# A transformer layer on one core: the first stage ordered by hand, seven v tiles and a Q block moved into later dense groups

## The chip, the cores and the metric

The kernel runs on 1 core of one Trainium2 chip, in one launch. The metric is device time in microseconds of the whole program. One profiled execution of the program comes with a trace of every instruction on the five engines: PE (TensorE), DVE (VectorE), ACT (ScalarE), POOL (GpSimd) and SP (SyncE, which issues nearly all DMAs here).

## The reference

```python
# S = 2048 rows, D = 512, H = 32 heads of 16, F = 1792; all float32
xn  = layernorm(x)                              # eps 1e-5, no scale, no shift
q, k, v = heads(xn @ wqkv)                      # wqkv: 512 x 1536
p   = softmax(q @ k.T / 4)                      # per head, 2048 x 2048
A   = merge(p @ v) @ wo
B   = gelu_tanh(xn @ w1 + b1) @ w2 + b2
out = x + A + B
```

## The kernel before

**Numbers.** Operands of the dense products are split into a float16 high and low half, each scaled by a power of two found from the largest absolute value of a weight; a product is three matmuls per slice of 128 (`PAIRS`). A dense 512-wide result is therefore 12 products (q, k, v, hidden layer), or 21 for half of the second MLP matrix.

**Attention in units.** Heads come in eight groups of four (`NG`), queries in four blocks of 512 (`NQB`), keys in 16 tiles of 128: 8 x 4 x 16 = 512 units (`NU`). Unit `u` has two sides that run 20 units apart (`LEAD`). The score side (`s_half`, four times a unit) multiplies four 32-column tiles of queries with 512 keys and takes the row maximum on DVE into `mt`; this is only there to find each row's maximum. After 16 units (`s_end`, `store`, `put`) the negated maxima go through DRAM into two spare rows of the stacked queries `qst`; the matching rows of the stacked keys `kst` hold 1024 (`MROW`). The value side (`e_half`, `v_half`) makes the transposed scores with the maximum already subtracted, takes the exponential on ACT and multiplies with `vv`, the v rows with a column of ones for the sum. `stacks` loads `kst` and `qst` from `qk_d` in DRAM, where the projections stored them.

**PE in halves.** In the steady part the array is used in two halves of 64 rows and four columns of tiles. While `v_half` runs on one row half, `dense` puts products of the current `Group` on the other: `pace` says how many half-width parts a unit's half gets, `FAST` 8, `MEAN` 7, `SLOW` 6. A 12-product group is 48 parts: three units at FAST, four at SLOW. Groups are given by generators: `rest` (the q and k projections of head blocks `m` = 1 to 3), then `mlp` (hidden groups at SLOW, sums at MEAN), then `tail` (the product with `wo`). Before unit 20, where no value side runs yet, `unit` calls `burst`, which puts `LFILL` whole products on the full array twice a unit.

**First stage.** Up to unit 16 the code is not run by `unit`: `stats` makes the mean and inverse deviation of four x tiles and normalises them, `transpose_x` turns x into `xt`, `prep_qk` and `prep_v` scale and split weights, `project` makes q and k of head block 0, `v_proj` all 16 v tiles, and `tile_and_unit` interleaves one score unit with one v tile (two score blocks, six products, two blocks, six products). `measure` finds the largest absolute values of w1, w2 and wo, half a 512 KB chunk at a time; chunks rotate over three buffers (`chunk`, `fetch`). In this stage the order on each engine is the planner's; from `rest` on (`manual_schedule`) it is the order of the code. SP's DMA issues stand in one queue, in order.

**Banks.** PSUM has eight banks in named lists: `S` three for scores, `T` three for transposed scores and early work, `D` one for dense groups, `V` one.

**Weights of the MLP.** `prepare` runs beside the units from 17 on: it finishes `measure`, forms scales, loads every chunk again, and splits it on POOL (`split_steps`, three operations a chunk) into `w1_d`, `w2_d` and `wo_s`.

Of the kernel before, what the change touches and what calls it, by code (L numbers as in the profile page):

```python
# [17 lines left out]
P = 128  # L18
# [14 lines left out]
MEASURE = (3, 0, 1, 2)  # L33
# [4 lines left out]
LFILL = 6  # L38
# [5 lines left out]
MROW = 1024.0  # L44
W = 2 * P
# [3 lines left out]
def layer_kernel(ctx: ExitStack, tc: tile.TileContext, x, wqkv, wo, w1, b1, w2, b2, out):  # L49
# [7 lines left out]

    const = pool(ctx, "const")
# [18 lines left out]
    ones_row = const.tile([2, P], F16, name="ones_row")  # L77
    nc.vector.memset(ones_row, MROW)

# [4 lines left out]
    def clear(i):  # L84
        for b in range(NQB):
            for p in range(2):
                for st in (kst[i][p][b], qst[i][p][b]):
                    nc.gpsimd.memset(st.bitcast(F32), 0.0)
                for a in range(2):
                    nc.sync.dma_start(kst[i][p][b][64 * a + 62:64 * a + 64, :].rearrange("r (b n) -> r b n", n=P),  # L90
                                      ones_row.unsqueeze(1).to_broadcast([2, 4, P]))
# [254 lines left out]
    def v_half(u, a):  # L346

        t, kt = divmod(u, 16)
        g, qb = divmod(t, NQB)
        if kt == 0 and a == 0:  # L350
            pv_of[t] = hold("V", "S")
        pv = pv_of[t][0]
        r = slice(64 * a, 64 * a + 64)
        for h in (2, 3, 0, 1):
# [91 lines left out]
    def dbank():  # L446
        turn[0] += 1
        if pos[0] < LEAD:
            return banks("T"), None
# [62 lines left out]
    def prep_qk(m, wf, bank, ready_w):  # L512
# [5 lines left out]
        yield from scales(am, 2, bank, box) if m < 2 else spread_scales(m, am, box)  # L518
        inv, fac = box
        wh = ph.tile([P, 2, 2, NC, P], F16, name="wqk_h", bufs=2)  # L520
        for w in (1, 0):
            (split if w and m == 0 else split_pool)(wh[:, w, 0], wh[:, w, 1], wf[w], inv[:, w:w + 1])
            yield
        nc.vector.tensor_tensor(sexp[:, m:m + 1], fac[:, 0:1], fac[:, 1:2], op=ALU.mult)
# [14 lines left out]
    def project(m, w, sb, wh, bank, early=False):  # L539
# [6 lines left out]
        def finish(pj):  # L546
# [21 lines left out]
            put()  # L568

# [9 lines left out]
    def v_proj(t, wh, bank):  # L579
        pj = bank()  # L580
        n = 0
        for c in range(NC):
            for i, j in PAIRS:
                nc.tensor.matmul(pj, xt[:, i, c, t * P:(t + 1) * P], wh[j][:, c, :], start=(n == 0), stop=(n == 11))  # L584
                n += 1
                yield 1.0
        nc.scalar.activation(vv[:, t, 0:H * VW].rearrange("p (h e) -> p h e", e=VW)[:, :, 0:DH],
                             pj.rearrange("p (h d) -> p h d", d=DH), AF.Copy)

# [78 lines left out]
    def unit(gen):  # L668
# [4 lines left out]
        if u == LEAD and cur[0] is not None:  # L673
            burst(gen, cur[0].left())
        pos[0] += 1
# [37 lines left out]
    with ExitStack() as st1:  # L713
# [23 lines left out]

        b1_s = const.tile([P, NF], F32, name="b1_s")
# [6 lines left out]
        amx = work.tile([P, 16, 2], F32, name="amx")  # L745
        fac1 = []
# [17 lines left out]
        def stats(sb):  # L764
# [20 lines left out]
            for i in range(4):  # L785
                v = xs[4 * sb + i]
                if sb and i >= 2:
# [12 lines left out]
        def transpose_x(sb, c):  # L800
            cs = slice(sb * QB, (sb + 1) * QB)
            pt = vbank()
            for i in range(4):
                nc.tensor.transpose(pt[:, i * P:(i + 1) * P], xs[4 * sb + i][:, c * P:(c + 1) * P], ident)
            nc.scalar.activation(xt[:, 0, c, cs], pt, AF.Copy)
            if sb and c % 2:
# [5 lines left out]
            if c == NC - 1:  # L812
                for t in range(4 * sb + 8, min(4 * sb + 12, NT)):
                    load_x(t)
# [19 lines left out]
        def measure():  # L834

            for n in range(16):
                v = fetch(n)
                for k in range(2):
                    absmax(amx[:, n, k:k + 1], v[:, 2 * k:2 * k + 2, :] if n < 7 else v[:, k, :])
                    yield  # L840
# [7 lines left out]
        def tile_and_unit(t):  # L848

            if t < 8:  # L850
                keep_x(t)
            v = v_proj(t, wvh, vbank)
            for k in range(2):
                s_half(t, 2 * k)
                s_half(t, 2 * k + 1)
                some(v, 6)
            s_end(t)
            run(v)
# [16 lines left out]
        def pq3(gen):  # L875
            for _ in range(3):
                next(gen)
                yield

        clear(0)  # L880
        ln, pq, pv = stats(0), prep_qk(0, wfs[0], sbank, ready_w), prep_v()
        warm(WARM[0])
        some(ln, 5)
        some(pq, 2)
        warm(WARM[1])
        some(ln, 3)
        some(pq, 1)
        some(ln, 2)
        weave(pq3(pq), ln)
        transpose_x(0, 0)  # L890
        warm(WARM[2])
        some(pq, 1)
        transpose_x(0, 1)
        warm(WARM[3])
        transpose_x(0, 2)
        transpose_x(0, 3)
        run(pq)
        run(stats(1))
        for w in (1, 0):
            run(whole(project(0, w, 0, ready_w[0], lambda: (vbank(), None), True)))  # L900
        for w in (1, 0):
            stacks(0, w, [0])
        free[:] = ["T", "D", "T", "V", "T"]
        for c in range(NC):
            transpose_x(1, c)
        some(pv, 2)
        for sb in range(1, NQB):
            ln = stats(sb + 1) if sb < 3 else iter(())
            for w in (1, 0):
                pj = whole(project(0, w, sb, ready_w[0], lambda: (vbank(), None)))  # L910
                for n in range(3):
                    some(pj, 4)
                    some(pv, 1)
                    if sb == 2:
                        some(ln, 3)
                run(pj)
            run(pv)
            for w in (1, 0):
                stacks(0, w, [sb])
            wfs.append(load_qk(sb))  # L920
            if sb == 1:
                clear(1)
            for j in range(4):
                tile_and_unit(4 * sb - 4 + j)
                some(ms, MEASURE[sb])
                if sb == 1:
                    some(ln, 4)
                elif sb == 2:
                    transpose_x(3, j)
            if sb == 1:  # L930
                for c in range(NC):
                    transpose_x(2, c)
        pq = prep_qk(1, wfs[1], sbank, ready_w)
        for j in range(4):
            some(pq, 2)
            tile_and_unit(NT - 4 + j)
            some(ms, MEASURE[0])
        run(pq)
# [6 lines left out]
        def rest():  # L945
            for t in range(8, NT):
                later(2 + 3 * (t - 8), lambda t=t: keep_x(t), True)
            for k in range(8):
                later(8 + 4 * k, lambda k=k: stacks(1, 1 - k // 4, [k % 4]), True)
            for m in range(1, 4):  # L950
                while m not in ready_w:
                    yield None
                if m < 3:
                    by_slots(prep_qk(m + 1, wfs[m + 1], sbank, ready_w))
# [17 lines left out]
        def prepare():  # L972
# [5 lines left out]
            nc.vector.tensor_reduce(am[:, 9:10], amx[:, 14:16, :], axis=AX.XY, op=ALU.max)  # L978
            box = []
# [5 lines left out]
            nc.vector.reduce_max(gs[:, 0:1], fac[:, 0:8], axis=AX.X)  # L985
# [39 lines left out]
        ctx.enter_context(tc.manual_schedule(engines=ORDERED))  # L1025
# [8 lines left out]
    def mlp():  # L1034
# [35 lines left out]
        def hidden_group(s, f):  # L1070
# [6 lines left out]
            def hidden(hp):  # L1077
# [8 lines left out]
                         dbank, hidden, pace=SLOW)  # L1086
# [184 lines left out]
```

## Time and profile before

| | us |
|---|---|
| three runs | 1472.27, 1474.18 (median), 1475.49 |
| the profiled execution | 1471.34 |
| its span, first to last instruction | 1469.5 |
| first score maximum starts | 37.4 |
| first maximum of unit 16, 20, 80 | 110.9, 124.9, 301.2 |
| last maximum ends | 1396.9 |

Times in a window or a timeline row count from the span's start. A windows row gives the stretch, its length, and the busy time and count of instructions in it, then granted clock of TensorE (1.00 is full), mean share of the 16 DMA engines and GB/s. A groups row gives line, engine, operation, out<-in and count, then busy time and mean ns of one, then idle time of the engine just before them with what ended most of it. A row of the chain of waits gives start, length, engine, tile and line. An instruction that straddles a window's edge is counted in both. L291 is the score matmul, L292 the maximum; L195 is the helper `tiled`/`product` with all half-array matmuls; L343 the exponential; L485 whole-array products of a Group; L584 and L587 the v tile and its read; L734 the weight maximum; L804 to L811 the transposes of x; L177 and L178, L967 to L969 splitting on POOL.

### The profile page before, as it was taken

What the parts mean: (1) busy time and instruction counts of PE and PEld (TensorE: products, weight loads), DVE (VectorE), ACT (ScalarE), POOL (GpSimd) and SP (SyncE); (2) the same over time, 40 slices, a digit from 0 to 9 for tenths busy, and PEclk for the clock granted to TensorE, in tenths of its full rate; (3) what the DMA queues carried; (4) which work ended last, traced back from release to release, by engine and by line L of the source; (5) the groups of instructions that cost most, each with busy time, mean ns of one, the idle gap of its engine ahead of it and who ended that gap; (6) DMA issues with size and microseconds to landing.
All of it is one profiled execution on the core that took longest, in us unless ns stands there. A gap on an engine that the chain in (4) does not pass through costs nothing.

```text
span 1469.5 us, 87300 instructions
## 1 busy us (share of the span) xinstructions
PE 1445.6 (98%) x39753; PEld 928.6 (63%) x39753; DVE 1363.0 (93%) x2340; ACT 1230.0 (84%) x2326; POOL 737.5 (50%) x846
## 2 busy tenths in 40 slices
PE   8999989999999999999999999999999999999998
PEld 4434656666666666666666666666666666666674
DVE  7799998999999999999999999999999999999913
ACT  5325877899899999999998999999999999998884
POOL 4113598747766536556553655456475545551100
PEclk9999999999999999999999999999999999999999
DMA  6466457544111211121121211121101211102342
GB/s 205 154 185 176 137 183 241 171 127 117 59 42 44 88 51 37 45 58 53 38 66 45 63 44 45 30 75 50 56 26 54 78 37 35 29 24 73 112 130 102
DMA packets 118023, 124.30 MB, mean 85 GB/s; under 512 B 29080, under 2 KB 89624, under 8 KB 117652
## 3 DMA queue, kind: packets, MB, share of 16 engines
q1 hardware_dynamic: 117652, 118.72, 26.5%
q8 instruction: 310, 5.08, 1.4%
q14 instruction: 61, 0.50, 0.1%
HBM read 80.87 MB, written 37.60 MB: 81 GB/s over the span
## 4 chain that ended last, share of the span: by engine, by line
PE 90%; POOL 4%; DVE 3%; DMA 1%; issue 1%; ACT 1%; SPq 0%; DVEq 0%; POOLq 0%; ACTq 0%
PE pV L195 25%; PE pD L195 23%; PE pT L195 19%; PE pS L291 18%; PE pS L195 2%; PE pT L584 1%; DVE mt L292 1%; PE pV L584 1%; PE pS L485 1%; POOL wsp L969 1%; PE pT L485 1%; DVE amx L734 0%; PE pD L584 0%; PE pD L485 0%; POOL t L1053 0%
## 5 line engine op out<-in xcount | busy, mean ns | idle before, releaser
L292 DVE TENSOR_REDUCE mt<-pS 128x1 f32<-128x512 f32 x2048 | 1270.0, 682 | 35.5 <-PE pS L291 21.6
L343 ACT ACTIVATE pe<-pT 128x512 f32<-128x512 f32 x2048 | 1105.1, 599 | 133.8 <-PE pS L291 64.7
L195 PE MATMUL pV<-pe,vv 64*32 64x512 f32 x8192 | 1088.1, 599 | 0.5 <-issue 0.2
L195 PE MATMUL pT<-qst,kst 64*32 64x512 f16 x8192 | 658.8, 376 | 3.1 <-ACT pe L343 2.1
L291 PE MATMUL pS<-kst,qst 62*32 62x512 f16 x8192 | 621.6, 378 | 6.2 <-DVE mt L292 4.6
L195 PE MATMUL pD<-xb,wc 64*32 64x512 f16 x5376 | 372.0, 374 | 0.0
L195 PE MATMUL pD<-w_s,g 64*32 64x512 f16 (+1 forms) x6144 | 361.4, 348 | 0.6 <-POOL g L1054 0.4
L291 PEld LDWEIGHTS <-qst 62*32 62x32 f16 x8192 | 250.2, 92 | 136.6 <-issue 38.2
L195 PEld LDWEIGHTS <-kst 64*32 64x32 f16 x8192 | 250.3, 93 | 98.3 <-issue 12.7
L195 PEld LDWEIGHTS <-g 64*32 64x32 f16 x6144 | 197.4, 92 | 87.2 <-POOL g L1055 1.1
L195 PEld LDWEIGHTS <-wc 64*32 64x32 f16 x5376 | 178.3, 91 | 98.0
L195 PEld LDWEIGHTS pV<-pe,vv 64*32 64x32 f32 x8192 | 171.0, 105 | 6.6 <-PE pV L195 2.5
L1082 POOL TENSOR_SCALAR hh<-hh,fac,b_s 128x512 f32<-128x512 f32 x56 | 43.0, 768 | 223.9 <-ACT hh L1080 217.8
L195 PE MATMUL pD<-xt,wqk_h 64*32 64x512 f16 x1920 | 128.7, 375 | 2.3 <-issue 1.5
L1109 POOL TENSOR_TENSOR xa<-xa,yt 128x512 f32<-128x512 f32 x32 | 41.1, 1284 | 89.6 <-ACT yt L1107 89.6
L397 POOL TENSOR_TENSOR osb<-osb,rb 128x512 f32<-128x512 f32 x31 | 39.9, 1287 | 89.3 <-DMA rb<-den_d 86.7
L195 PEld LDWEIGHTS <-wqk_h 64*32 64x32 f16 x1920 | 60.8, 92 | 31.0 <-issue 5.9
L1053 POOL TENSOR_TENSOR t<-t,hh 128x512 f32<-128x512 f32 x56 | 71.8, 1282 | 4.7
L1060 POOL TENSOR_TENSOR t<-t,hh 128x512 f32<-128x512 f32 x56 | 71.8, 1281 | 4.7
L1055 POOL TENSOR_TENSOR g<-t,g 128x512 f16<-128x512 f32 x56 | 65.2, 1164 | 4.6
L1146 DVE SCALAR_TENSOR_TENSOR ac<-pS,gs,ac 128x512 f32<-128x512 f32 x20 | 14.4, 743 | 52.0 <-PE pS L195 40.3
L1058 POOL TENSOR_TENSOR t<-hh 128x512 f32<-128x512 f32 x56 | 58.2, 1040 | 4.1
(144 smaller groups left out, 908.1 us busy)
## 6 DMA issues: line engine op xcount, KB each, us to landing
wch<-in_B_w_dram SPq DMA_DIRECT2D x28, 512.0 KB
wc<-w_d SPq DMA_DIRECT2D x56, 256.0 KB
qk_d<-stg SPq DMA_DIRECT2D x32, 256.0 KB
rb<-den_d SPq DMA_DIRECT2D x31, 256.0 KB
w_d<-wsp SPq DMA_DIRECT2D x28, 256.0 KB
kst<-qk_d SPq DMA_DIRECT2D x128, 48.0 KB
qst<-qk_d SPq DMA_DIRECT2D x128, 48.0 KB
xs<-in_A_x_dram SPq DMA_DIRECT2D x16, 256.0 KB
```

Of the source, the lines that this page charges most:

```text
L195: p = nc.tensor.matmul(*args, **kw)
L291: nc.tensor.matmul(s[32 * j:32 * j + 32], qs[p][qb][r, c:c + 32], ks[p][kb][r, :], start=True, stop=True)
L292: nc.vector.reduce_max(mt_of[t][:, n, qt, kb:kb + 1], s, axis=AX.X)
L343: nc.scalar.activation(pe, st, AF.Exp, scale=factor(exp_scale, sexp[0:1, g // 2:g // 2 + 1]))
L397: pooled((1280, lambda: nc.gpsimd.tensor_tensor(osb, osb, rb, op=ALU.mult)), (620, lambda: nc.gpsimd.tensor_scalar(ot[:, 0], osb, 1.0, 0.0 ...
L485: nc.tensor.matmul(self.bank, lhs, rhs, start=start, stop=self.last and self.over())
L1053: (1280, lambda: nc.gpsimd.tensor_tensor(t1, t1, hh, op=ALU.mult)),
L1055: (1160, lambda: nc.gpsimd.tensor_tensor(g[:, 1, f, :], t1, g[:, 0, f, :], op=ALU.subtract)),
L1058: pooled((1040, lambda: nc.gpsimd.tensor_tensor(t1, hh, hh, op=ALU.mult)), (620, lambda: nc.gpsimd.tensor_scalar(t1, t1, 1.0, 1.0 / GELU_A ...
L1060: (1280, lambda: nc.gpsimd.tensor_tensor(t1, t1, hh, op=ALU.mult)),
L1082: later(1, lambda: pooled((690, lambda: nc.gpsimd.tensor_scalar(hh, hh, scale, bias, op0=ALU.mult, op1=ALU.add)), (0, lambda: gelu(hh, g, ...
L1109: add = lambda: nc.gpsimd.tensor_tensor(xa, xa, yt, op=ALU.add)
```

## The change

- `manual_schedule` is entered at the start: the order of the code holds on every engine in the first stage too.
- The first stage's sequence is written out anew. A score unit (`scores`) emits its four score blocks in a row, then a list of fills. Transposes of an x block go tile by tile over four banks (`turn_all`) or a column block at a time (`turn_x`).
- `v_rows` makes nine of 16 v tiles in the stage. The other seven (`MOVED`), and the Q projection of block 3, are groups at the head of `rest`, at FAST. The q and k weights of block `m` = 1 are prepared from unit 19 on, those of 2 and 3 five units after the preceding block's groups begin.
- `kst` is filled with 1024 by POOL memsets (two float16 of 1024 in one float32, `MROW2`), in place of zeros and two 2-row DMAs for each of its tiles, 32 in all.
- `measure` takes the sum of absolute values with ACT (Abs with an accumulator, in place) where DVE took the largest; 20 of its 32 steps are in the first stage, before 24. `prepare` scales the sums down.
- Normalising x: block 1's first two tiles and all of blocks 2 and 3 on POOL, one tile of block 1 on ACT; before, two tiles of every block from 1 on were on ACT and the rest on DVE. The low halves of `xt` of blocks 2 and 3 are all made on POOL (before, every second one).
- `S` has four banks and `T` two until unit 20.
- `LFILL` goes from 6 to 3, and five of nine hidden groups run at FAST.

```diff
-LFILL = 6
+LFILL = 3
+MOVED = 7
...
+    ctx.enter_context(tc.manual_schedule(engines=ORDERED))
...
     def clear(i):
...
-                for st in (kst[i][p][b], qst[i][p][b]):
-                    nc.gpsimd.memset(st.bitcast(F32), 0.0)
-                for a in range(2):
-                    nc.sync.dma_start(kst[i][p][b][64 * a + 62:64 * a + 64, :]...)
+                nc.gpsimd.memset(kst[i][p][b].bitcast(F32), MROW2)
+                nc.gpsimd.memset(qst[i][p][b].bitcast(F32), 0.0)
...
+        if u == LEAD:
+            free_banks["T"].insert(0, free_banks["S"].pop(0))
...
+        def abssum(dst, v):
+            nc.scalar.activation(v, v, AF.Abs, accum_out=dst)
+            given("act", 650)
...
-                if sb and i >= 2:
+                if sb > 1 or (sb and i < 2):
+                    nc.gpsimd.tensor_scalar(v, v, mv[:, i, 0:1], sd[:, 2, i:i + 1], op0=ALU.subtract, op1=ALU.mult)
+                elif sb and i == 3:
...
-            if sb and c % 2:
+            if sb > 1 or (sb and c % 2):
...
+        def v_rows():
+            for t in range(NT - MOVED):
+                yield from v_proj(t, wvh, vbank)
+
+        def scores(u, *fill):
+            if u < 8:
+                keep_x(u)
+            for n in range(4):
+                s_half(u, n)
+            for gen, n in fill:
+                some(gen, n)
+            s_end(u)
...
+        turn_all(0)
+        run(pq)
+        run(ln)
+        clear(1)
...
+        run(side(0, 1))
+        run(l1)
+        run(side(0, 0))
...
+        turn_all(1)
+        some(pv, 1)
+        free[:] = ["T"]
+        free_banks["S"].append(free_banks["T"].pop(0))
+        ln, vs = stats(2), v_rows()
+        (side(1, 1) with three steps of pv; run(pv); some(ln, 5); side(1, 0) with four of ln; run(ln))
+        some(vs, 12)
+        ln = stats(3)
+        scores(0, (vs, 3), (turn_x(2, 0), 1), (vs, 3), (turn_x(2, 1), 1))
...
+        scores(1, (vs, 3), (turn_x(2, 2), 1), (vs, 3), (turn_x(2, 3), 1))
+        some(ln, 2)
+        scores(2, (side(2, 1), 13))
+        some(ln, 4)
+        fetch(0)
+        scores(3, (side(2, 0), 13))
+        run(ln)
+        scores(4, (vs, 3), (turn_x(3, 0), 1), (ms, 1), (vs, 3), (turn_x(3, 1), 1))
...
+        scores(5, (vs, 3), (turn_x(3, 2), 1), (ms, 1), (vs, 3), (turn_x(3, 3), 1))
+        scores(6, (side(3, 1), 13), (ms, 1))
+        scores(7, (vs, 8), (ms, 1))
+        for u in range(8, 16):
+            scores(u, (vs, 4), (ms, 1), (vs, 4), (ms, 1))
...
+            later(3, lambda: by_slots(prep_qk(1, wfs[1], sbank, ready_w)), True)
+            for t in range(NT - MOVED, NT):
+                yield v_group(t)
+            yield project(0, 0, 3, ready_w[0], dbank, True, lambda: later(4, lambda: stacks(0, 0, [3]), True))
...
-                         dbank, hidden, pace=SLOW)
+                         dbank, hidden, pace=FAST if (HF * s + f) % 9 in (0, 2, 4, 6, 8) else SLOW)
```

(The one line in brackets stands for a loop over those steps.)

More of the change, by code (lines that the diff above doesn't have):

```diff
@@ L448, in dbank @@
         if pos[0] < LEAD:
-            return banks("T"), None
+            return banks(free[turn[0] % len(free)]), None
         if pos[0] > NU:
@@ L904, in layer_kernel @@
[L904 to L938, printed above, removed]
+        turn_all(1)
+        some(pv, 1)
+        free[:] = ["T"]
+        free_banks["S"].append(free_banks["T"].pop(0))
+        ln, vs = stats(2), v_rows()
+        pj = side(1, 1)
+        for n in range(3):
+            some(pj, 4)
+            some(pv, 1)
+        run(pj)
+        run(pv)
+        some(ln, 5)
```

142 lines of the change are left out of this document (93 added, 49 removed).

## The prediction

> **What bounds the kernel now.** I read four views, in this order: the page (who is busy, what ended last), then one instruction counted in windows cut at the starts of score units, then all engines in the first stage's windows, then single rows. The granted clock is 0.99 or 1.00 in every window shown, so it enters no term.
>
> ```profile
> span 1469.5 us, 87300 instructions
> PE 1445.6 (98%) x39753; PEld 928.6 (63%) x39753; DVE 1363.0 (93%) x2340; ACT 1230.0 (84%) x2326; POOL 737.5 (50%) x846
> PE 90%; POOL 4%; DVE 3%; DMA 1%; issue 1%; ACT 1%; SPq 0%; DVEq 0%; POOLq 0%; ACTq 0%
> ...
> L292 DVE TENSOR_REDUCE mt<-pS 128x1 f32<-128x512 f32 x2048 | 1270.0, 682 | 35.5 <-PE pS L291 21.6
> ```
>
> PE carries the chain, but one operation keeps count of the program: each of 512 score units has four score blocks and four DVE maxima (L292). Its windows:
>
> ```profile
> core 0: us, DVE busy (x), PEclk, DMA share, GB/s
> 37.40:77.00 39.60, 20.81 (x32) 1.00 0.51 158
> 77.00:110.90 33.90, 20.19 (x32) 1.00 0.62 180
> 110.90:124.90 14.00, 10.03 (x16) 1.00 0.63 188
> 124.90:149.90 25.00, 20.19 (x32) 1.00 0.58 172
> 149.90:301.20 151.30, 131.97 (x208) 1.00 0.60 184
> 301.20:377.20 76.00, 73.78 (x120) 1.00 0.36 105
> 377.20:1352.60 975.40, 951.13 (x1542) 1.00 0.17 50
> 1397.00:1469.50 72.50, 0.00 (x0) 0.99 0.36 118
> ```
>
> Four in a count are one unit; the first maximum starts at 37.4, where the first window is cut. Units 0 to 15 (the first stage) take 73.5 us, 4.6 each; 16 to 19 take 3.5 each; 20 to 27 take 3.1; 28 to 79 take 2.91; 80 to 109 take 2.53; 110 to 494 (385 units; two maxima of 1542 straddle a cut) take 975.4/385 = 2.533, with DVE 97.5% in maxima. So the late program has next to no room, the first stage wastes some 2 us a unit, and 72.5 us follow the last maximum. What fills the first stage:
>
> ```profile
> core 0: us, PE busy (x) PEld busy (x) DVE busy (x) ACT busy (x) POOL busy (x), PEclk, DMA share, GB/s
> 37.40:77.00 39.60, 39.30 (x282) 16.30 (x282) 31.24 (x58) 15.43 (x29) 5.77 (x5) 1.00 0.51 158
> 77.00:110.90 33.90, 33.15 (x235) 11.38 (x233) 32.44 (x60) 6.09 (x11) 4.82 (x5) 1.00 0.62 180
> ```
>
> PE is full in both halves, DVE nearly full in the second, ACT and POOL idle: work taken from PE and DVE there shortens the stage.
>
> **The change, part by part.** Prices come from the chain of waits (first five rows) and the groups of the first stage's window:
>
> ```profile
> 37.35 0.32 PE pT L584
> 52.88 2.59 PE pT L485 x12
> 56.34 0.34 PE pS L291 x8
> 56.68 1.40 PE pV L584 x6
> 58.08 0.44 PE pT L804 x4
> ...
> L734 DVE TENSOR_REDUCE amx<-wch 128x1 f32<-128x512 f32 x24 | 15.1, 678 | 0.3 <-DMA wch<-in_B_w_dram 0.3
> L809 POOL TENSOR_TENSOR xt<-pf,xt 128x512 f16<-128x512 f32 x4 | 4.6, 1153 | 27.8 <-ACT pf L808 27.8
> L177 POOL TENSOR_SCALAR wq<-wq,inv 128x512 f32<-128x512 f32 x2 | 1.4, 690 | 26.4 <-issue 26.4
> L788 ACT ACTIVATE xs<-xs,sd 128x512 f32<-128x512 f32 x2 | 1.3, 706 | 0.0
> ```
>
> *The start.* The two clears lose 32 DMA issues on the one SP queue:
>
> ```profile
> 7.20 12.62 SPq L90 DMA_DIRECT2D kst<-ones_row  x16
> 21.83 0.39 SPq L548 DMA_DIRECT2D qk_d<-stg  x1
> ...
> 41.68 10.66 SPq L90 DMA_DIRECT2D kst<-ones_row  x16
> ```
>
> The projection store behind them left at 21.83. That frees the queue, but the first maximum at 37.4 is not set by it alone: PE must still turn x block 1, make two projections (5.2 us) and a v tile, and DVE in its new written order has the halves of wvh and the statistics of block 2 ahead of the first maximum. Following DVE's new list from the projections' end, at about 0.7 for each 512-wide operation and 1.2 for each half of wvh, I put the first maximum at 35.3: an estimate, 2.1 us gained (bounds 0 and 5). The second clear, on POOL now ahead of block 1's normalisation, still lies before that list.
>
> *PE in units 0 to 15.* Seven of 16 v tiles (12 products each) and one Q projection leave. A lone product between score blocks costs 0.32, six in a row 1.40, so a product is 0.216 and a switch 0.1; a 12-product projection is 2.6; four score blocks are 0.7; four transposes 0.44. New units 0, 1, 4, 5: 0.7+1.4+0.9 = 3.0 each; 2, 3, 6: 0.7+2.6 = 3.3; 7 to 15: 0.7+8x0.216+0.1 = 2.5. Sum 12+9.9+22.5 = 44.4 us where PE was busy 72.5. DVE needs 64 maxima at a spacing of about 0.61 (four in a 2.5 us unit) = 39 us, plus an estimated 5 us (eight operations near 0.65) of statistics and stores, and loses 24 weight maxima (15.1 us), five normalisations and four low halves of x: it fits beside PE.
>
> *Waits that come instead.* Order is now as written, on every engine. POOL normalises four tiles of x block 2 (4x0.69 = 2.8 us) just before unit 0 turns them: PE waits about 2 us. For block 3 POOL first has the low half of the Q store of unit 3 (1.15 us, after two ACT copies), then 2.8 us: unit 4's transposes, with v products, scores and therefore the maxima queued behind them on PE, wait about 4 us. I take 6 together (bounds 1 and 12: nothing if POOL runs ahead, twice if both chains slip).
>
> *POOL against DVE.* Where POOL is busy a small DVE operation can hang, as these rows of the timeline show beside the same form at rest:
>
> ```profile
> 10.69 0.14 DVE L140 TENSOR_SCALAR fac<-sc_c 128x2 int32<-128x2 int32 x1
> 196.56 2.13 POOL L969 TENSOR_TENSOR wsp<-wch,wsp 128x1024 f16<-128x1024 f32 x1
> 196.85 1.88 DVE L164 TENSOR_SCALAR fac<-am_c 128x2 int32<-128x2 int32 x1
> ```
>
> The statistics of block 3 have six such operations while POOL does low halves of 1.15 us; half of that at a time, mostly off PE's path: I take 2 us (bounds 0 and 7). The Trainium skill, SBUF — State Buffer, section SBUF: two separate sides, says that a VectorE operation in a two-port mode or with two SBUF inputs and a GpSimd operation lock each other out for the whole instruction; the rows above agree. By that rule alone, each of the six waiting a full low half, this term would be 7 instead of 2 and the forecast 1464.
>
> *ScalarE measures weights.* 20 half-chunks in the stage at about 0.7 (the nearest rows are L788's 706 ns), twice in units 8 to 15: with a v read of 0.6 in two of three units ACT has 1.8 us of work in 2.5, nothing on the path, if the loads come; that is a rival below. Stage sum: 35.3+44.4+6+2 = 87.7 for unit 16, where it was 110.9: **-23 us** (bounds -32 and -9).
>
> *Units 16 to 19.* Three fill products a half instead of six, no weight maximum on DVE: 0.7+6x0.216 = 2.0 on PE, 2.5 on DVE: 10.4 instead of 14.0, **-3.5** (bounds -4 and 0).
>
> *Units 20 to 27.* DVE's weight maxima in 20 to 23 go; ACT gets one measuring step per unit until unit 27 (12 left).
>
> ```profile
> L343 ACT ACTIVATE pe<-pT 128x512 f32<-128x512 f32 x2048 | 1105.1, 599 | 133.8 <-PE pS L291 64.7 <-PE pT L195 63.9 <-ACT pe L343 0.4
> L773 ACT ACT_TABLE_LOAD x1 | 1.3, 1283 | 0.7 <-PEq L1258 0.7
> L343 ACT ACT_TABLE_LOAD x1 | 1.3, 1283 | 0.6 <-DVE mt L292 0.6
> ```
>
> Four exponentials occupy ACT for 4x1105.1/2048 = 2.16 us, plus 0.7 plus a v read of 0.6 in three units = 3.05: ACT bounds these eight units, 24.4 us and the table load 1.3 = 25.7 against 25.0: **+0.7** (bounds -3 and +5).
>
> *Units 28 to 79.* v groups (until unit 38) and the projections run at eight parts a half, as before. The excess over 2.6 a unit, about 16 us in this stretch, comes with POOL's weight splitting and heavy DMA (share 0.60), which only start about five units later: **0** (bounds -8 and +6). Moved are 96 products: 24 go in units 16 to 19, then four a unit until 38. The new waits on a v read are covered: the seventh tile ends near unit 35 and is first multiplied after it. The Q block's two stores and four loads pass on SP near units 38 to 42 and are read from unit 48; the weight loads of the later projections start five units ahead of their use, beside steady work: nothing for both.
>
> *Units 80 to 494, the price.* Moving 96 products shifts the MLP from unit 80 to unit 110, and 31 of 56 hidden groups go from six to eight parts a half (three units instead of four). What a unit costs by pace, in undisturbed stretches (rows 1 and 2: 3 and 2 units of projections at eight; row 3: 8 units of hidden groups at six; rows 4 and 5: 8 units each of sums at seven):
>
> ```profile
> 277.20:285.05 7.85, 7.74 (x13) 1.00 0.74 222
> 293.29:298.50 5.21, 5.15 (x8) 1.00 0.90 281
> 321.21:341.39 20.18, 19.73 (x33) 1.00 0.44 122
> 504.65:524.95 20.30, 19.86 (x33) 1.00 0.29 89
> 767.65:788.11 20.46, 19.84 (x32) 1.00 0.15 44
> ```
>
> Eight: 13.06/5 = 2.61. Six: 2.52. Seven: 2.54 to 2.56. Units 80 to 109 go to 30x2.61 = 78.3 from 76.0, **+2.3**. Units 110 to 494 become 93x2.61+100x2.52+192x2.55 = 984.3 against 975.4: **+8.9** (bounds 0 and +17, the latter at 2.70 a unit). Groups then end at unit 110+93+100+192 = 495, before at 80+224+192 = 496, so the output products and the 72.5 us tail stay: **0** (bounds -1 and +3). The three extra small DVE operations in the scales cost 0.5 at rest: in the bounds.
>
> Sum: -23-3.5+0.7+0+2.3+8.9 = -14.6. The profiled execution took 1471.34 (span 1469.5 and 1.8 around it): 1456.7. The median of the three runs is 1474.18, 2.8 higher: 1459.6. I put **1459**.
>
> **The rivals.**
> - *Clean start* (0.16): POOL runs ahead, no lockouts, first maximum at 33: stage -32, units 28 to 79 -4, the rest as above: 1443. For it: PE's own work is 44 us. Against: the written order of POOL.
> - *Starved ScalarE* (0.09): units 8 to 15 use one 512 KB chunk each.
>
> ```profile
> 116.97 4.33 DMA wch<-in_B_w_dram
> ```
>
> If chunks came singly at 4.33, eight units take 34.6 instead of 20: +14.6, 1473, about no change. ACT would hold the v reads, and PE its banks. Against: three buffers, and 524 kB in 2.5 us is 210 GB/s where 281 were moved above.
> - *Dense pace becomes the bound* (0.07, slower): the first rows of pace eight come from picked stretches; units 28 to 79 as a whole cost 2.91. At 2.91 the 123 added units of pace eight cost 123x0.39 = 48 instead of 11: 1496. It decides from 2.73 a unit (the 26 us gained ahead of it, over 123 units above 2.52). Against: that stretch has a DMA share of 0.60 and the weight splitting, the MLP a share of 0.17 and none.
> - *Table loads* (0.03, slower): if Abs and Exp lay in different sets, units 16 to 27 would pay up to 12x2x1.283 = 31 us: 1490. Against: two loads in the whole program although Exp, Tanh and copies alternate. The Trainium skill, ScalarE: Activation LUTs, section Table sets, says abs is in every set; by that it costs nothing; no run shown yet has an Abs.
>
> **How the numbers follow.** My forecast has 0.65, its own range 1449 to 1468 from the terms' bounds taken together half-way. About 3 us (0.2%) is what measurement can tell from nothing. Faster: 0.65+0.16+0.02 of the starved case = 0.83; same 0.05 (starved); slower 0.07+0.03+0.02 = 0.12. The range 1441 to 1473 leaves out the two slower rivals and the low edge of the clean start, under 0.2.
>
> **What would show it.** Right: unit 16's first maximum near 88, with PE idle before transposes around units 0 and 4; maxima 2.6 us a unit from 8 to 15; ACT the releaser in units 20 to 27 at 3.0; about 2.6 in hidden groups at eight parts; same 72 us after the last maximum; two table loads. Wrong: unit 16 before 80 or after 97, a hidden pace above 2.7, or a longer tail.

## The result, and the profile after

The changed kernel is slower: 1497.13 us median (1495.73 to 1499.02), the kernel before beside it 1473.22 (1472.16 to 1475.49), ratio 1.0161 with a 95% interval from 1.0142 to 1.018. The profiled execution has a span of 1494.3 us, 24.8 above that of before. The head of its page, with the shares by engine of the chain and the maxima:

```profile
span 1494.3 us, 89118 instructions
PE 1442.6 (97%) x40674; PEld 945.1 (63%) x40674; DVE 1353.4 (91%) x2302; ACT 1246.1 (83%) x2383; POOL 763.2 (51%) x860
PE 88%; POOL 4%; DVE 3%; issue 2%; ACT 2%; DMA 1%; SPq 0%; DVEq 0%; POOLq 0%; ACTq 0%
L288 DVE TENSOR_REDUCE mt<-pS 128x1 f32<-128x512 f32 x2048 | 1280.0, 683 | 62.6 <-PE pS L287 42.9
```

TensorE is busy 3.0 us less in all, and the span is 24.8 us longer: PE stands idle where it did not before. The page alone does not say where. The maxima (now L288) do, in windows cut at the same units as before: units 0 to 7, 8 to 15, 16 to 19, 20 to 27, 28 to 79, 80 to 109, 110 to 494, and the stretch behind the last maximum.

```profile
core 0: us, DVE busy (x), PEclk, DMA share, GB/s
43.40:91.00 47.60, 19.72 (x33) 0.78 0.36 111
91.00:111.80 20.80, 19.57 (x33) 1.00 0.94 275
111.80:121.50 9.70, 9.65 (x17) 1.00 0.28 74
121.50:151.70 30.20, 20.57 (x33) 0.89 0.47 145
151.70:305.60 153.90, 131.38 (x208) 1.00 0.53 166
305.60:384.50 78.90, 76.58 (x120) 1.00 0.28 87
384.50:1377.80 993.30, 960.36 (x1541) 1.00 0.19 56
1423.10:1494.30 71.20, 0.00 (x0) 0.98 0.35 116
```

| stretch | before, us | after, us | difference | predicted |
|---|---|---|---|---|
| up to the first maximum | 37.4 | 43.4 | +6.0 | -2.1 |
| units 0 to 7 | 39.6 | 47.6 | +8.0 | |
| units 8 to 15 | 33.9 | 20.8 | -13.1 | |
| *to unit 16, together* | 110.9 | 111.8 | **+0.9** | **-23** |
| units 16 to 19 | 14.0 | 9.7 | -4.3 | -3.5 |
| units 20 to 27 | 25.0 | 30.2 | **+5.2** | **+0.7** |
| units 28 to 79 | 151.3 | 153.9 | +2.6 | 0 |
| units 80 to 109 | 76.2 | 78.9 | +2.7 | +2.3 |
| units 110 to 494 | 975.1 | 993.3 | **+18.2** | **+8.9** |
| unit 495 to the end of the span | 117.0 | 116.5 | -0.5 | 0 |

Three terms miss: the first stage by 24 us, units 20 to 27 by 4.5, the long MLP stretch by 9.3. Each has rows of its own.

**The first stage.** These are GpSimd's instructions on the x tiles (duration minimum/median/maximum in ns, then first and last start), and the waits of TensorE up to 43.4 us (first row) and from there to 112 (second row); columns: us in total, times, longest:

```profile
L810 POOL TENSOR_SCALAR xs<-xs,mv,sd x10: 2070/2072/2330, 22.0 to 74.9; 128x512 f32<-128x512 f32 x10
```

```profile
PE pT L834 <- POOL xs L810: 5.4, 2, 4.4
...
PE pD L834 <- POOL xs L810: 14.3, 8, 2.5
```

One normalisation takes 2.07 us where the prediction had 0.69. The first pair holds up block 1 before the first maximum, and the eight of blocks 2 and 3 make PE wait 14.3 us in units 0 to 7: 19.7 in all. The windows of all engines (PE, PEld, DVE, ACT, POOL) show what else that costs. The first lies before the first maximum, the next two around the waits of blocks 2 and 3; then come units 8 to 15, and units 0 to 15 together:

```profile
20.00:30.00 10.00, 3.94 (x16) 3.14 (x16) 4.32 (x9) 3.83 (x8) 4.38 (x2) 0.67 0.47 123
43.40:60.20 16.80, 9.14 (x62) 4.13 (x62) 7.63 (x16) 4.76 (x10) 12.38 (x8) 0.70 0.30 94
68.40:83.60 15.20, 8.30 (x60) 3.74 (x57) 4.94 (x9) 4.16 (x9) 10.81 (x8) 0.66 0.52 165
91.00:111.80 20.80, 20.69 (x190) 7.59 (x190) 19.71 (x34) 13.06 (x37) 0.00 (x0) 1.00 0.94 275
43.40:111.80 68.40, 52.33 (x414) 20.41 (x414) 44.93 (x82) 28.15 (x70) 28.02 (x18) 0.85 0.54 161
```

With PE busy 39 to 55% of a window, its granted clock averages 0.66 to 0.70. Windows cut where the clock changes have it either half or full:

```profile
47.23:57.47 10.24, 5.35 (x29) 2.19 (x29) 1.22 (x3) 2.17 (x4) 7.53 (x5) 0.50 0.38 115
57.47:71.12 13.65, 11.09 (x89) 4.47 (x87) 12.29 (x27) 4.44 (x9) 6.50 (x6) 1.00 0.43 131
```

The same three fill products, first before block 2's waits, at full clock, then behind four of them, at half:

```profile
43.69 0.81 PE L591 MATMUL pT<-wvh,xt 128*128 128x512 f16 x3 [0.56 <-ACT stg L566]
53.41 1.49 PE L591 MATMUL pT<-wvh,xt 128*128 128x512 f16 x3
```

So a wait is paid twice: PE stands still, and then works at little more than half its speed. Units 0 to 7 kept PE busy 52.33-20.69 = 31.6 us; the prediction's sum for the same work is 24.4. The Trainium skill, TensorE: Matmul & The Clock Gate, section Part 1: The HAM clock gate, says that the gate falls to half after an idle window of about 3.4 us; the trace agrees with the half (0.50 us a product instead of 0.22 to 0.27). No single wait for x tiles in units 0 to 7 is longer than 2.5 us, so here the clock fell without an idle time of that length. Units 8 to 15, where nothing waits, take 2.60 each as forecast.

The first maximum came 8 us after the forecast, and a small part of that lies before the normalisations. Two small DVE operations of block 1's statistics, while GpSimd cleared the stacks (rows of both engines' timelines):

```profile
15.80 0.31 POOL L86 MEMSET kst<- 128x256 f32 x1
...
19.60 0.31 POOL L87 MEMSET qst<- 128x256 f32 x1
```

```profile
17.71 2.22 DVE L794 TENSOR_SCALAR sd<-mv 128x4 f32<-128x4 f32 x1
18.92 1.02 DVE L798 TENSOR_SCALAR sd<-mv 128x4 f32<-128x4 f32 x1
```

Each takes 0.17 us or less where the trace has it for blocks 0 and 2; here both end within 0.05 us of the last clear. The lengths can't be added: the two overlap, and between them stands a weight maximum that needs 1.2 us in any case. The delay that is left is about 0.9 us, an estimate from the run with the normalisation off GpSimd, where the pair is done 1.4 us after its start, and here 2.2.

**Units 20 to 27.** One step of ScalarE's measuring found no chunk loaded:

```profile
122.28 0.63 ACT L756 ACTIVATE wch<-wch 128x512 f32<-128x512 f32 x1 [5.46 <-DMA wch<-in_B_w_dram]
122.81 0.19 ACT L756 ACTIVATION_READ_ACCUMULATOR wch<-wch 128x1 f32 x1
...
124.11 1.28 ACT L339 ACT_TABLE_LOAD   x1
```

SP's queue had issued that chunk late, behind other steps of the stage:

```profile
113.57 0.37 SPq L317 DMA_DIRECT2D m_d<-mhl  x1
115.13 2.77 SPq L322 DMA_DIRECT2D qst<-m_d  x4
118.01 0.38 SPq L745 DMA_DIRECT2D wch<-in_B_w_dram  x1
```

ScalarE stood 5.46 us, and the exponentials of unit 20 are behind it (the table load of the third row is the one ahead of them); PE stood with it (clock 0.80 from 121.5 to 138.8). The middle row is a small cost that no step of the prediction had: the sum of an Abs is read out by an instruction of its own.

**The MLP.** All engines in units 110 to 494, of before and of after:

```profile
377.40:1352.50 975.10, 974.49 (x29183) 653.37 (x29182) 959.31 (x1614) 890.27 (x1695) 524.15 (x596) 1.00 0.17 50
```

```profile
384.50:1377.80 993.30, 989.50 (x29952) 671.59 (x29947) 969.03 (x1613) 898.53 (x1709) 569.41 (x643) 1.00 0.19 56
```

PE was busy 99.9% of this stretch before. After, it carries 769 more matmuls, as many as the 96 moved products make at eight row-tile matmuls each, and 15.0 us more of busy time; the other 3.2 us agree with one new wait, for a softmax denominator in unit 123, whose load stands on SP behind stack loads:

```profile
DVE dn L383 <- DMA dn<-den_d: 3.2, 1, 3.2
```

By the pace of the unit (told from its dense matmuls), the 93 units of eight parts took 2.66 us on average, 2.62 without unit 123, where the units of six that they replace took 2.51: 14 us. The units of six and seven took 2.53 and 2.57 for 2.51 and 2.56 before: 4 us. The medians of six and seven did not move (2.51 and 2.54); there are 22 units above 2.75 us, and before there were 3.

### The profile page after: what moved, and what is told of

Same layout as the page of the kernel before. It is cut to its first block, busy times and chain, and to the rows that moved or that the text cites. A ratio compares the mean times of both kernels' runs of the same rounds, so it can differ in the third digit from the quotient of the medians.

```text
span 1494.3 us, 89118 instructions
## 1 busy us (share of the span) xinstructions
PE 1442.6 (97%) x40674; PEld 945.1 (63%) x40674; DVE 1353.4 (91%) x2302; ACT 1246.1 (83%) x2383; POOL 763.2 (51%) x860
## 4 chain that ended last, share of the span: by engine, by line
PE 88%; POOL 4%; DVE 3%; issue 2%; ACT 2%; DMA 1%; SPq 0%; DVEq 0%; POOLq 0%; ACTq 0%
PE pD L191 25%; PE pV L191 24%; PE pT L191 18%; PE pS L287 16%; PE pS L191 2%; POOL xs L810 1%; PE pT L591 1%; DVE mt L288 1%; ACT pe L339 1%; PE pS L482 0%; POOL t L1127 0%; DMA wq<-in_A_wqkv_dram 0%; POOL g L1129 0%; DMA wch<-in_B_w_dram 0%; POOL xt L842 0%
## 5 line engine op out<-in xcount | busy, mean ns | idle before, releaser
L288 DVE TENSOR_REDUCE mt<-pS 128x1 f32<-128x512 f32 x2048 | 1280.0, 683 | 62.6 <-PE pS L287 42.9
L191 PE MATMUL pT<-qst,kst 64*32 64x512 f16 x8192 | 677.2, 377 | 6.2 <-ACT pe L339 2.9
L287 PE MATMUL pS<-kst,qst 62*32 62x512 f16 x8192 | 614.3, 379 | 5.8 <-DVE mt L288 5.4
L191 PE MATMUL pD<-xb,wc 64*32 64x512 f16 x5376 | 361.3, 375 | 0.0
L191 PEld LDWEIGHTS <-kst 64*32 64x32 f16 x8192 | 255.0, 93 | 98.1 <-issue 20.8
L191 PEld LDWEIGHTS <-wc 64*32 64x32 f16 x5376 | 174.8, 92 | 83.4 <-issue 0.4
L191 PEld LDWEIGHTS pV<-pe,vv 64*32 64x32 f32 x8192 | 181.1, 105 | 12.0 <-issue 6.8
L191 PE MATMUL pD<-xt,wqk_h 64*32 64x512 f16 x2400 | 161.3, 375 | 3.6 <-issue 3.6
L191 PEld LDWEIGHTS <-wqk_h 64*32 64x32 f16 x2400 | 78.8, 92 | 36.9 <-issue 6.7
```

The source lines that it names most:

```text
L191: p = nc.tensor.matmul(*args, **kw)
L287: nc.tensor.matmul(s[32 * j:32 * j + 32], qs[p][qb][r, c:c + 32], ks[p][kb][r, :], start=True, stop=True)
L288: nc.vector.reduce_max(mt_of[t][:, n, qt, kb:kb + 1], s, axis=AX.X)
```

## The experiments

Two questions are put. What ate the first stage: GpSimd's slow normalisation (theory A), or, its rival, the written order, in which every engine waits for the slowest? And what made the MLP longer: the pace of eight parts in itself, or that PE has no free time there, so that moved work costs late what it saves early (theory D)? "Unit 16 at 96.8" means that its first maximum starts there.

**The normalisation as a multiply-add.** In the changed kernel:

```
-  nc.gpsimd.tensor_scalar(v, v, mv[:, i, 0:1], sd[:, 2, i:i + 1], op0=ALU.subtract, op1=ALU.mult)
+  nc.gpsimd.tensor_scalar(v, v, sd[:, 4, i:i + 1], sd[:, 2, i:i + 1], op0=ALU.add, op1=ALU.mult)
```

> The changed kernel with one operation of the ten POOL normalisations written another way: add of the negated mean instead of subtract of the mean, then the same multiplication; two per-partition operands as before. Theory A (the form of the operation sets its price: 2.07 us for subtract-multiply, 0.77 us for add or multiply forms, as the hidden layer's scale-and-bias on POOL takes): the ten operations take about 0.77 us, PE waits for them about 4 us instead of 21, unit 16 starts near 90 instead of 111.8, total near 1497 - 22 = 1475. Rival B (two per-partition operands, or the port shared with DVE, make it 2.07): operations stay at 2.07, total 1497. Rival C (the order written by hand stalls anyway, another wait takes over): operations at 0.77, but unit 16 stays above 105 and the total above 1490.

```profile
L810 POOL TENSOR_SCALAR xs<-xs,sd x10: 762/770/1022, 22.3 to 60.8; 128x512 f32<-128x512 f32 x10
```

1482.99 against 1475.91, ratio 1.0048 [1.0026, 1.0071]. With `add` in place of `subtract` (it adds the negative mean) the instruction takes 0.77 us, PE's waits for it in units 0 to 15 fall from 14.3 to 4.0 us, and unit 16 comes at 96.8 instead of 111.8. That is theory A; 15 us of the first stage were one operator. Rival B of the expectation falls as well, since the fast form has two per-partition operands and the same neighbours. Unit 16 is still 7 us behind the 90 expected: the first maximum came at 39.2, and the clock averaged 0.86 in units 0 to 7. The total is above before, and 8 us above what was expected: the later terms are larger than the prediction had them.

**The normalisation off GpSimd.** Blocks 1 to 3 normalised on DVE and ScalarE as in the kernel before:

```
-  if sb > 1 or (sb and i < 2):
-      nc.gpsimd.tensor_scalar(v, v, ...)
-  elif sb and i == 3:
+  if sb and i >= 2:
       nc.scalar.activation(v, v, ...)      # the other tiles: DVE
```

> The changed kernel with the normalisation of x blocks 1 to 3 on the engines of before: two tiles of a block on DVE (0.54 us each), two on ACT (two operations of 0.71 each); none on POOL. Theory A: PE no longer waits 21 us for POOL, unit 16 near 90, total near 1475, like the other form. Rival C (the written order stalls in itself): unit 16 above 105, total above 1490. If this one is faster than the add form by more than 3 us, POOL's queue (a store's low half ahead of the normalisation) is a cost of its own.

1479.04 against 1475.91, 1.0031 [1.001, 1.0052]; unit 16 at 90.8. All engines in units 0 to 7, and from the first maximum to unit 16:

```profile
40.80:69.90 29.10, 25.66 (x220) 11.30 (x221) 26.12 (x51) 18.37 (x38) 10.65 (x9) 1.00 0.59 182
40.80:90.80 50.00, 46.41 (x410) 18.88 (x411) 45.92 (x85) 31.56 (x75) 10.65 (x9) 1.00 0.73 221
```

The clock is back at 1.00 and PE's busy time at 46.4 us, near the prediction's 44.4, with the written order untouched: the rival falls. In units 0 to 7 PE was busy 25.7 us with 220 matmuls, where the changed kernel has 31.6 with 224. The four missing ones are worth about 0.9, so some 5 us, an estimate, go with the lower clock. The total is 4.0 us below that of the add form, but the intervals overlap: that GpSimd's queue is a cost of its own, as the expectation would read this, is not shown. The stage now saves 20.1 us, and yet the kernel is not faster. From unit 16 to the last maximum it takes 27.7 us more than the kernel before.

**Eight parts in the kernel before.** Nothing moved, only the pace of 5 in 9 hidden groups of the later spans:

```
-  dbank, hidden, pace=SLOW)
+  dbank, hidden, pace=FAST if s > 1 and (HF * s + f) % 9 in (0, 2, 4, 6, 8) else SLOW)
```

> The kernel before with the faster pace alone, in the third to eighth part of the MLP: of the 42 hidden groups there, five of nine get eight parts a half. Nothing else is changed, so the first stage and the weights' preparation are as before and the dense groups finish about 23 units earlier. Pace theory: 23 groups x 3 units at 2.61 instead of 2.52, +6 us in those, nothing gained from finishing early while 512 units bound the end: last maximum about 1403 instead of 1397, total +4 to +8. Rival (the pace itself is free, the changed kernel's MLP is slow for another reason): last maximum within 2 us of 1397 and total the same.

1487.18 against 1475.91, 1.0076 [1.0047, 1.0105]. Units 80 to 494 took 1060.9 us in its profile, before 1051.3: +9.6, and the medians differ by 11.3, above the 4 to 8 expected. A further 4.5 us of its profile arose behind unit 495, and 5.0 before unit 80, where the two kernels have the same code: two profiles can differ by 5 us without a cause in it. The groups finish earlier, and nothing uses the units that this frees. Four of these, without any dense product:

```profile
1357.58:1367.11 9.53, 9.53 (x196) 3.71 (x190) 9.53 (x17) 8.46 (x17) 1.39 (x2) 1.00 0.31 85
```

A unit is here 2.38 us, and PE reads busy throughout with 49 matmuls a unit, where the MLP of the changed kernel has 78. So PE's busy share of 99.9% does not show that it has no room; DVE is full in these units too. The run shows that the pace costs by itself; it leaves open which of the two causes acts in the changed kernel, where the faster groups make room for moved work.

**Abs on ScalarE alone.** In the kernel before, with the scales made from the sums and everything else as it was:

```
+  def abssum(dst, v):
+      nc.scalar.activation(v, v, AF.Abs, accum_out=dst)
...
-  absmax(amx[:, n, k:k + 1], ...)
+  abssum(amx[:, n, k:k + 1], ...)
```

> One part of the change alone: the kernel before, with ScalarE measuring the weights (Abs with an accumulator, and the scales made from sums) and nothing else. If DVE's weight maxima cost time before (24 of 0.61 in the first stage, 8 in units 16 to 23), units 8 to 15 go from 4.2 toward PE's 3.5 (-6), units 20 to 23 from 3.4 toward 3.0 (-1 to -2), all later units stay: total -4 to -8. Rival (PE held these units anyway and ACT waits for the chunks instead, as it did 5.5 us at unit 20 of the changed kernel): within 3 us of before, or slower.

```profile
76.40:105.10 28.70, 28.70 (x228) 10.32 (x227) 21.76 (x40) 18.96 (x53) 4.85 (x5) 1.00 0.75 224
```

1469.77 against 1474.40, 0.996 [0.9945, 0.9975]: this is faster than both kernels. In units 8 to 15 DVE's 32.4 us of 33.9 become 21.8 of 28.7, PE fills the whole stretch, and unit 16 comes 5.8 us earlier. Units 20 to 23, where 1 to 2 us were expected, gained nothing (14.0, before 13.7). What remains at the end of the span is 1.5 in the profile and 4.6 in the medians.

**The two late waits mended.** The kernel with the normalisation off GpSimd, chunk loads one step further ahead, and the stack loads of the next groups spread over the units before the MLP too:

```
-  while len(loads) <= min(k + 1, 31):
+  while len(loads) <= min(k + (2 if k < 12 else 1), 31):
...
+          more_stacks()      # in the loop over the units before the MLP
```

> The changed kernel with the normalisation on DVE and ACT, and two waits taken away: weight chunks are asked for two ahead instead of one while ScalarE measures, and the loads of the third head group's stacks start when they may and not only once the MLP runs. Expected if these waits cost what the traces show: no 5.4 us wait of ACT at unit 20 and no DVE wait of 3 us for a denominator at unit 123: units 20 to 27 from 29.3 to 26, units 110 to 127 3 us less, total 1479 - 6 = 1473 on the same footing. Rival (the waits only move, since the chunks come no faster): total within 2 us of the version without these two edits.

```profile
102.60:128.50 25.90, 23.00 (x624) 13.77 (x624) 21.20 (x35) 23.27 (x52) 0.00 (x0) 1.00 0.46 149
128.50:287.80 159.30, 146.87 (x4183) 94.79 (x4179) 140.93 (x255) 125.21 (x235) 106.98 (x97) 0.99 0.52 161
366.70:1357.70 991.00, 990.12 (x29952) 670.47 (x29943) 969.09 (x1613) 898.09 (x1709) 571.15 (x643) 1.00 0.18 55
```

1475.89 against 1474.40, 1.0005 [0.9985, 1.0024]: no change from before. Units 20 to 27 (first row) take 25.9 us, the prediction's 25.7, now that no chunk is late, and the MLP (third row) 991.0, with PE busy in all but 0.9 us of it. With every wait that was found mended, the change gains 17.9 us up to unit 16 and 4.4 in units 16 to 19, and loses 0.9, 8.0, 2.7 and 15.9 in the four stretches to unit 494: +27.5 against -22.3. The 8.0 are those of units 28 to 79 (second row), and not all of them need a cause: the run with the pace alone, which has the code of before there, took 154.9. Nor is PE full in them, with 146.9 us of 159.3.

**Nothing moved.** The same kernel, with the seven v tiles and the Q block back in the first stage, the preparation of the next weights (`pq1`) beside them, and the hidden groups at six parts, but for the first two:

```
-MOVED = 7
+MOVED = 0
-LFILL = 3
+LFILL = 6
...
-      scores(u, (vs, 4), (ms, 1), (vs, 4), (ms, 1))
+      scores(u, (vs, 8), (pq1, 1), (ms, 1), (vs, 8), (pq1, 1), (ms, 1))
...
-  dbank, hidden, pace=FAST if (HF * s + f) % 9 in (0, 2, 4, 6, 8) else SLOW)
+  dbank, hidden, pace=FAST if HF * s + f < 2 else SLOW)
```

> The kernel of the run with two waits taken away, but with nothing moved: all 16 v tiles and the Q block of block 3 are made in the hand-ordered first stage, the burst before unit 20 is six products as before, and all but two hidden groups run at six parts as before. Theory D (PE has no free time anywhere, so the 96 moved products cost as much later as they save first): unit 16 comes 96 x 0.216 = 21 us later than in that run (near 111), units 110 to 494 fall back from 995 to 976 and units 80 to 109 by 2: total the same within 4 us. Rival (moving them is a net gain or loss): it differs by 8 us or more either way.

```profile
377.90:1354.20 976.30, 974.97 (x29168) 653.82 (x29165) 959.30 (x1612) 890.75 (x1696) 528.08 (x598) 1.00 0.17 51
```

1478.35 against 1474.40, 1.0031 [1.0014, 1.0047], 2.5 us above the kernel that moves. Unit 16 is 15.4 us later (108.4 against 93.0), the MLP 14.7 us shorter, the last maximum 2.2 us earlier, and the stretch behind it 2.8 us longer. Theory D holds in what it costs: moving 96 products out of the first stage only changes the place where they are paid. That PE had no free time for them is its reason, and this run does not test the reason. This kernel measures on ScalarE as well, and is still no faster than before: what the written order, with the other parts of the change, makes of the first stage without the moves is 3.3 us worse than the former order with the same measuring (unit 16 at 108.4 against 105.1).

**Which form is slow.** In the changed kernel, GpSimd's normalisation split into two instructions, in three ways: block 1 (L811, L812) multiplied by 1 and subtracted the mean, then multiplied and added 0; block 2 (L814, L815) subtracted and multiplied by 1, then multiplied twice; block 3 (L817, L818) added 0 and subtracted, then multiplied and subtracted an immediate 0.

> The changed kernel with each POOL normalisation cut into two operations, in other forms: block 1 multiply by 1, subtract the mean (per-partition), then multiply by the per-partition factor and add 0; block 2 subtract the mean first, multiply by 1, then two multiplications; block 3 add 0, subtract the mean, then multiply and subtract 0. If subtraction as such is slow on POOL, every first operation takes near 2 us and block 3's second too, the other second ones 0.69; if only subtraction in the first place is slow, block 2's first alone; if it is the pair of two per-partition operands, none.

```profile
L814 POOL TENSOR_SCALAR xs<-xs,mv x4: 1997/1997/2002, 44.3 to 52.6; 128x512 f32<-128x512 f32 x4
L815 POOL TENSOR_SCALAR xs<-xs,sd x4: 693/694/697, 46.4 to 54.7; 128x512 f32<-128x512 f32 x4
L817 POOL TENSOR_SCALAR xs<-xs,mv x4: 2001/2001/2009, 70.6 to 82.8; 128x512 f32<-128x512 f32 x4
L818 POOL TENSOR_SCALAR xs<-xs,sd x4: 2002/2002/2002, 72.7 to 84.9; 128x512 f32<-128x512 f32 x4
L811 POOL TENSOR_SCALAR xs<-xs,mv x2: 1992/2000/2009, 20.0 to 23.1; 128x512 f32<-128x512 f32 x2
L812 POOL TENSOR_SCALAR xs<-xs,sd x2: 687/824/961, 22.1 to 25.2; 128x512 f32<-128x512 f32 x2
```

Each of the four forms with a `subtract` takes 2.0 us, whether it stands first or second and whether its operand is a pointer or a number; of the two without, one takes 0.69, the other 0.69 and 0.96 in its two instances. The program took 1514.92 in its one run.

**The clears without DMA.** The Abs kernel, its stacks filled by GpSimd alone (the two mask rows come from the value of the fill instead of a DMA from a row of constants):

```
-  for st in (kst[i][p][b], qst[i][p][b]):
-      nc.gpsimd.memset(st.bitcast(F32), 0.0)
-  for a in range(2):
-      nc.sync.dma_start(kst[i][p][b][64 * a + 62:64 * a + 64, :]..., ones_row...)
+  nc.gpsimd.memset(kst[i][p][b].bitcast(F32), MROW2)
+  nc.gpsimd.memset(qst[i][p][b].bitcast(F32), 0.0)
```

> Two parts of the change on the kernel before: Abs on ScalarE, and the stacked keys' spare rows filled by POOL memsets, so that 32 small DMAs leave SP's queue (12.6 us of it ahead of the first projection store, 10.7 us in the first stage). If the queue held the first scores: the store leaves before 21.8, the first maximum comes 2 to 3 us before 37.5 and the total falls to about 1467. Rival (PE's own list sets the first score, since v tiles fill the time while it waits): first maximum and total within 1 us of Abs alone, 1469.8.

1473.34 against 1473.75, 0.9997 [0.9978, 1.0017]. The first maximum does come earlier, at 32.1 against 37.5, but unit 4 is at 57.8 and unit 16 at 111.5, 6.4 us behind the Abs kernel: from the first maximum to unit 16 there are now 79.4 us instead of 67.6, with unit 3 at 14.2 instead of 6.1 and unit 7 at 13.2 instead of 9.6. The earlier start of the scores was given back inside the stage, and neither the total expected nor the rival's unchanged first maximum came. Why the planner put it so is open.

**More measuring in the first stage.** The kernel of the clears, with all 32 steps before unit 16:

```
-MEASURE = (3, 0, 1, 2)
+MEASURE = (3, 1, 2, 2)
```

> As the run with both parts, and ScalarE measures all but none of the weights inside the first stage: one step a unit from unit 0 and two from unit 4 (32 in all, 24 before), so no measuring falls beside the exponentials of units 20 to 23. If those eight steps (0.75 us each) cost time there: units 20 to 23 from 3.5 to 3.2, total -1 to -2. Rival (ACT then waits for chunks in the first stage, holding the v reads): no gain, or units 0 to 15 later by 1 to 3 us.

```profile
ACT wch L735 <- DMA wch<-in_B_w_dram: 10.1, 7, 2.5
```

1480.80 against 1473.75, 1.0045 [1.003, 1.006]. Units 20 to 23 get faster (2.89 us each instead of 3.58), but unit 16 comes at 117.6 instead of 111.5, and ScalarE waits 10.1 us for chunks. The prediction's rival of a starved ScalarE shows in that wait, in a kernel that asks for it. It explains the loss in part at most: 4.5 of the 6.1 us arise before the first maximum (36.6 instead of 32.1), where 1.8 of the 10.1 lie.

## Why the prediction was wrong

*The first stage, -23.* The step that failed is "POOL normalises four tiles of x block 2 (4x0.69 = 2.8 us)". It took the duration of a TENSOR_SCALAR of the same shape (L177, multiply and add) for one that subtracts, and no row of before had such a form on GpSimd. At 2.07 us, PE waits 14.3 us in units 0 to 7 where the prediction has 6, above its bound of 12, and 5.4 more before the first maximum. A second step failed with it: "The granted clock is 0.99 or 1.00 in every window shown, so it enters no term" was true of the kernel before, where PE was full, and false as soon as PE waited. PE's work in units 0 to 7 became 31.6 us instead of 24.4, and about 5 of these 7 go with the clock. Both steps are shown by the two normalisation runs, in which unit 16 comes at 96.8 and 90.8. That 90.8 is only 3 us behind the prediction's 87.7 is in part luck: the first maximum is 5.5 us late in that run (40.8 instead of 35.3), and the way from there to unit 16 is 2.4 short. So the estimate for the start failed too. In the changed kernel it is 8.1 us late, 4 of which go with the subtraction (39.2 with `add`); what the others are is not settled. DVE held up by GpSimd was priced at 2 us, in block 3's statistics; there one operation took 0.91 us instead of 0.16, and the rows above show another 0.9 us in block 1's, ahead of the first normalisation, where the prediction's order for the start has nothing of it. The term for units 8 to 15 was right. That for units 16 to 19 was nearly so: four units of 2.5 us are 10.0 and not the 10.4 written there, and 9.7 were measured.

*Units 20 to 27, +0.7.* The rival of a starved ScalarE was put in units 8 to 15, where the loads kept up (275 GB/s). It came in unit 20, as a single late chunk: SP, which issues in order, had the mask rows' store and loads ahead of it. The sum for these units, 25.7, came out at 25.9 with the load earlier.

*Units 110 to 494, +8.9.* This term is mis-sized: 18.2, of which 15.9 are left once the denominator's wait is gone. The price of a unit at pace eight was right (median 2.62, and 2.60 with that wait gone; the forecast 2.61). What failed is holding the other paces at 2.52 and 2.55 as in the picked stretches: over the whole stretch their means became 2.53 and 2.57, through slow units, and the wait in unit 123 was in no term. Of the 9.3 us missed, the other paces make 4.4, the wait 3.4 and pace eight 1.1. The prediction says itself that the late program has next to no room, and the moved work was paid there nearly in full: 96 products of 0.216 are 20.7 us, and 2.7 + 15.9 = 18.6 were paid after unit 80. That PE has no time left for them would explain it, but it is argued: the busy share reads full in units without dense products too.

*The rest.* The tail, two table loads and units 80 to 109 were right; units 28 to 79 lie inside their bounds in the changed kernel (+2.6), and above them in the one with the two waits mended (+8.0 against +6), by less than two profiles of the same code differ. The rival of dense pace gave 1496, close to the time measured, but for another reason: its 2.91 us a unit did not come about. The clean start's 1443 counts from the profiled 1456.7; from the forecast of 1459 it would be 1446. The rival of table loads is refuted; the Trainium skill, ScalarE: Activation LUTs, section Table sets, with abs in every set, agrees with the trace's two loads.

*What stays open.* Which steps of the start make the first maximum late without the subtraction; why the MLP has more slow units; and whether units 28 to 79 give back more than two profiles of the same code differ. The changed kernel with all hidden groups at six parts, which would have priced the pace in it directly, gave no time.

## What to carry to other kernels

Before moving work off a busy stretch, price it where it goes, over the whole of that stretch and not in picked units: here nearly 20 us saved early were paid again late. A busy share near 100% is a warning, not the price. Price an instruction from a row with the same operators, not the same shape alone, and where no such row exists put the bound a factor of three away. In a change of several parts try each alone: here the one part that took work off DVE without moving PE's was worth 0.4% alone, and the whole change lost 1.6%.

## What the runs showed of the hardware

- On GpSimd, TENSOR_SCALAR of 128x512 in float32 took 2.0 us with a `subtract` in either place (2.07 with two per-partition operands) and 0.69 us with multiplies alone, or multiply and add (L177 in the prediction); adding the negated operand and multiplying took 0.77.
- Plain MEMSETs on GpSimd, not only operations that read, stood beside small DVE operations with records of 2.22 and 1.02 us, which are 0.17 elsewhere in the trace and ended here with the last MEMSET; the delay that was left is about 0.9 us.
- With PE busy 39 to 55% over 10 to 17 us the granted clock was 0.66 to 0.70 on average, 0.50 or 1.00 at a time, and a 512-wide product took 0.50 us instead of 0.22 to 0.27. In units 0 to 7 no single wait for x tiles was longer than 2.5 us.
- In units without a dense product PE read busy throughout with 49 matmuls a unit, and in the MLP with 78: its busy share did not tell the two apart.
- ScalarE's accumulated sum costs an ACTIVATION_READ_ACCUMULATOR of 0.19 us behind each 0.63 us ACTIVATE.
